# Half-array pairs in two bank-swapping phases for the dense products and transposes of an attention + mixer kernel

## The chip, the cores and the metric

The kernel runs on one core of a Trainium2 chip. The metric is the device time of one execution in microseconds; for the kernel before, the median of three runs is 702.48 us (701.95 to 702.92). The engines are named as the profile names them: PE is TensorE, the 128 x 128 array that multiplies a stationary matrix, loaded from 128 partitions, with a moving one of up to 512 columns into one of eight banks of PSUM (PEld is the loading); DVE is VectorE, ACT ScalarE, POOL GpSimd, and SP the queue that issues most DMAs.

## What is computed

Two blocks read the same normalized tokens `xn` (2048 x 512) and are added to `x`: a memory-augmented linear/softmax attention over four segments of 512 tokens, 32 heads of 16, and a mixer MLP with 1792 hidden columns.

```python
def _A_ref(x, wq, wk, wv, wo, beta):      # per segment s of 4, L = 512
    logits = einsum("bhqd,bhkd->bhqk", qs, ks) * scale + mask
    p = softmax(logits); a_dot = einsum("bhqk,bhkd->bhqd", p, vs)
    pq = phi(qs)                            # phi(t) = t + 1 if t > 0 else exp(t)
    a_mem = einsum("bhld,bhde->bhle", pq, M) / (einsum("bhld,bhd->bhl", pq, z)[..., None] + 1e-6)
    o = g * a_mem + (1.0 - g) * a_dot
    M = M + einsum("bhld,bhle->bhde", phi(ks), vs); z = z + einsum("bhld->bhd", phi(ks))
    ...
    return o @ wo
def _B_ref(x, w1, b1, w2, b2):
    return gelu(layernorm(x) @ w1 + b1) @ w2 + b2
x = A_x; xn = layernorm(x)
return x + _A_ref(xn, ...) + _B_ref(xn, ...)
```

## The kernel before

The work is cut into 16 units: segment s (of 4) times group g (of 4, eight heads each); unit i is s, g = divmod(i, 4). Large products are made of fp16 halves: a number is split into a high part and a remainder, and three products (high x high, high x low, low x high) are added in PSUM. `split3` (L469) does that for a full 128-row contraction in KT = 4 steps, 12 products for each result.

The jobs that the change and the prediction speak of:

- `T` (`qk_proj`, L469): query or key of a unit, 12 full-array products of 512 columns. Behind it ACT and DVE read the bank and split it into `hl`, five DMAs on SP send it to DRAM (`qd`, `kd`) and back into the stacked tiles `qst`, `kst`.
- `M` (`m_jobs`, L594 on PE, L601 on DVE): the score maxima. The eight heads of a unit lie in the two 64-row halves of the array, so the products come in pairs, one in each half, into two banks, and run at the same time. The maxima go to `mc`; `R` (`m_row`, L609) transposes them.
- `S` (`s_jobs`, L634 on PE, L639 on ACT): the scores again, in the same pairs, and their exponentials into `pt`. `pv` (L663) multiplies these with the values, in four strips of 32 columns of the array; `K` (`kv`, L573) sums the memory in the same strips. `Qd` (`a_mem`, L542) applies the memory.
- `V` (`v_nat`, L469), values of a segment, and `out` (L788), the output product: 12 full-array products of 512 columns for each 128 tokens.
- `D` (`d_jobs`, L469): first MLP product, for 256 tokens and 128 hidden columns 12 full-array products of 256 columns; DVE reads the result at L729. `e` (`e_part`, L769): second MLP product, already as half-array pairs. [...] 
- Transposes through PE with an identity: the tokens (`ln_tr`, L455), the keys (`pk_nat`, L505), the maxima (L609), the row scales (`ratio`, L428), each 128 x 128 or, for the maxima, 128 x 32.

Nothing here is scheduled at run time. `streams()` lists the jobs by kind, a long string `ORDER` names, letter by letter, from which list the next job comes, and each engine gets its instructions in that order. A second string, `BANKS`, gives the PSUM bank of each `dense()` call, one digit each. [...]

```python
ps = dense(), dense()                      # m_jobs: a pair, one product in each half of the rows
for b, p in enumerate(ps):
    r = slice(64 * b, 64 * b + KM)
    T.matmul(p[:, o:o + n], stk[i, 0][r, t, P * qb:P * qb + P], stk[i, 1][r, t, :n], start=True, stop=True)
```

## Time and profile before

| | us |
|---|---|
| median of three runs | 702.48 |
| the profiled execution | 701.74 |
| its span, first to last instruction | 700.0 |
| PE busy | 681.6 (97%) |
| PE busy, first 50 us | 40.0 |
| DVE busy | 536.2 (77%) |
| ACT busy | 515.4 (74%) |
| POOL busy | 349.5 (50%) |
| granted TensorE clock, mean | 0.995 |

A row of a group reads: line, engine, operation, what it writes <- what it reads, shape and count | busy us, mean ns of one | idle us of the engine before it, and what ended that. `64*128` is the part of the array that a product uses (rows x columns), `64x512` its moving operand. A row of the timeline reads: start, length, engine, line, operation; equal neighbours are merged with their count. Products overlap in the array, so their mean is longer than the distance between their starts. A row of stretches gives the busy time of PE, PEld, DVE, ACT and POOL, then the granted clock, the share of the DMA engines and GB/s.

### The profile page before, as it was taken

To read this page: it belongs to the slowest core of one execution; us is meant where nothing else is said; L and a number is where in the kernel's file an instruction comes from. 1 tells how busy PE (TensorE), PEld (TensorE's weight loads), DVE (VectorE), ACT (ScalarE), POOL (GpSimd) and SP (SyncE) were. 2 spreads that over 40 slices of the span, in tenths; PEclk is the share of its full clock that TensorE was granted. 3 is DMA by queue.
4 is the path that set the end of the run, shared out by engine and by line. 5 is a ranking of instruction groups with operands and counts; after the bars stand their busy time and mean duration, and the time that the engine had idled before them with its cause. 6 is when DMAs were issued, how large, how long until landed. Compare 5 with 4: busy or idle time off the path is not lost.

```text
span 700.0 us, 16681 instructions
## 1 busy us (share of the span) xinstructions
PE 681.6 (97%) x6213; PEld 395.4 (56%) x6213; DVE 536.2 (77%) x1734; ACT 515.4 (74%) x954; POOL 349.5 (50%) x532
## 2 busy tenths in 40 slices
PE   7799999999999999999999999999999999999997
PEld 6355556575554555666454456566454556556653
DVE  5699979797795858889689786979679585969533
ACT  6879897779785768667794698765886586887870
POOL 5276767465533435555434446354443345465652
PEclk9899999999999999999999999999999999999999
DMA  9796123230404022323113322041121204241001
GB/s 280 222 252 182 33 67 89 68 86 4 121 3 122 31 78 62 78 47 77 48 48 109 94 59 76 18 107 46 42 69 46 93 2 107 77 111 29 4 2 61
DMA packets 51790, 55.11 MB, mean 79 GB/s; under 512 B 4782, under 2 KB 40636, under 8 KB 51708
## 3 DMA queue, kind: packets, MB, share of 16 engines
q1 hardware_dynamic: 49404, 49.84, 25.6%
q0 software_dynamic: 2304, 4.20, 3.6%
q8 instruction: 49, 0.80, 0.4%
q14 instruction: 33, 0.27, 0.1%
HBM read 36.99 MB, written 17.04 MB: 77 GB/s over the span
## 4 chain that ended last, share of the span: by engine, by line
PE 71%; DVE 9%; ACT 8%; DMA 6%; POOL 2%; issue 2%; SPq 1%; POOLq 0%; ACTq 0%; DVEq 0%
PE ps L469 27%; PE ps L769 17%; PE ps L663 9%; PE ps L788 5%; PE ps L634 5%; PE ps L594 4%; DVE ps L601 3%; ACT pt L639 2%; DMA qd<-hl 1%; PE ps L542 1%; ACT hT L736 1%; DMA mhl<-in_B_b_dram 1%; ACT w1s L310 1%; SPq L251 1%; DMA wos<-in_A_wo_dram 1%
## 5 line engine op out<-in xcount | busy, mean ns | idle before, releaser
L601 DVE CUSTOM_DVE_ANT_0 ps<-ps,mask 128x512 f32<-128x512 f32 (+3 forms) x512 | 234.0, 524 | 10.1 <-PE ps L594 8.9
L639 ACT ACTIVATE pt<-ps,qkcs 128x512 f32<-128x512 f32 (+1 forms) x384 | 204.7, 626 | 26.2 <-PE ps L634 21.8
L769 PE MATMUL ps<-w2s,hT 64*128 64x512 f16 x1344 | 175.0, 375 | 0.6 <-DVE fence L772 0.5
L469 PE MATMUL ps<-xnT,w1s 128*128 128x256 f16 x1344 | 159.1, 273 | 0.7 <-DVE phq L499 0.4
L648 POOL TENSOR_SCALAR_AFFINE_SELECT pt<-pt 128x256 f32<-128x256 f32 x256 | 101.1, 426 | 107.5 <-ACT pt L639 107.3
L469 PEld LDWEIGHTS <-w1s 128*128 128x128 f16 x1344 | 128.6, 98 | 28.4 <-issue 10.3
L769 PEld LDWEIGHTS <-hT 64*128 64x128 f16 x1344 | 77.1, 94 | 54.6 <-issue 7.3
L745 POOL TENSOR_TENSOR hT<-hh,hT 128x512 f16<-128x512 f32 x64 | 68.0, 1062 | 75.0 <-ACT hT L744 75.0
L663 PE MATMUL ps<-pt,vt 128*32 128x256 f32 (+3 forms) x1024 | 77.3, 436 | 0.0
L729 DVE SCALAR_TENSOR_TENSOR hT<-ps,sc,sr 128x256 f32<-128x256 f32 x112 | 51.7, 478 | 30.1 <-PE ps L469 28.1
L601 DVE DVE_READ_ACCUMULATOR2_ANT mc<- 128x1 f32 x512 | 71.8, 140 | 0.0
L634 PE MATMUL ps<-qst,kst 50*128 50x512 f16 (+3 forms) x512 | 70.2, 298 | 0.7 <-DMA qst<-md 0.3
L594 PE MATMUL ps<-kst,qst 48*128 48x512 f16 (+3 forms) x512 | 67.4, 297 | 1.1 <-DMA qst<-qd 0.9
L744 ACT ACTIVATE hT<-hh 128x512 f16<-128x512 f32 x64 | 36.6, 573 | 39.9 <-POOL hh L743 39.5
L663 PEld LDWEIGHTS ps<-pt,vt 128*32 128x32 f32 x1024 | 30.5, 109 | 42.9 <-issue 33.4
L743 POOL TENSOR_SCALAR hh<-hT,sc 128x512 f32<-128x512 f32 x64 | 41.6, 651 | 25.0 <-ACT hT L736 23.2
L736 ACT ACTIVATE hT<-hT,b1t 128x256 f32<-128x256 f32 x112 | 46.4, 495 | 0.2
L489 DVE SCALAR_TENSOR_TENSOR hl<-ps,hl 128x512 f16<-128x512 f32 x32 | 22.1, 689 | 32.0 <-ACT phk L488 16.3
L469 PE MATMUL ps<-xnT,wks 128*128 128x512 f16 x192 | 46.0, 389 | 0.1
L469 PE MATMUL ps<-xnT,wqs 128*128 128x512 f16 x192 | 45.8, 390 | 0.2 <-DVE mc L601 0.2
L634 PEld LDWEIGHTS <-kst 50*128 50x128 f16 x512 | 27.8, 94 | 28.8 <-issue 13.6
L469 PE MATMUL ps<-wvs,xnT 128*128 128x512 f16 x192 | 44.0, 379 | 0.1
(220 smaller groups left out, 899.9 us busy)
## 6 DMA issues: line engine op xcount, KB each, us to landing
kd<-hl SPq DMA_DIRECT2D x48, 128.0 KB
kst<-kd SPq DMA_DIRECT2D x32, 192.0 KB
qd<-hl SPq DMA_DIRECT2D x48, 128.0 KB
qst<-qd SPq DMA_DIRECT2D x32, 192.0 KB
acc<-in_A_x_dram SPq DMA_DIRECT2D x16, 256.0 KB
acc<-in_B_b_dram POOLq DMA_DIRECT2D x16, 256.0 KB, 4.3
out_dram<-acc SPq DMA_DIRECT2D x16, 256.0 KB
xt<-in_A_x_dram SPq DMA_DIRECT2D x14, 256.0 KB
```

What stands on the lines that cost most here:

```text
L469: T.matmul(p, wsl(ws, k, a), xsl(xs, k, b), start=s0 and i == 0, stop=s1 and i == 3 * n - 1)
L594: T.matmul(p[:, o:o + n], stk[i, 0][r, t, P * qb:P * qb + P], stk[i, 1][r, t, :n], start=True, stop=True)
L601: V.tensor_tensor_reduce(p[:, o:o + n], p[:, o:o + n], mask[:, 512 - n:], 1.0, -3e38, OP.add, OP.max, mc[i][:, 4 * b + t, qb:qb + 1])
L634: T.matmul(p[:, o:o + n], stk[i, 1][r, t, P * kb:P * kb + P], stk[i, 0][r, t, P * kb:], start=True, stop=True)
L639: A.activation(e[:, OFF[kbs[0]]:OFF[kbs[0]] + o], p[:, :o], AF.Exp, scale=qkcs[:, 1, i % NG:i % NG + 1])
L648: G.affine_select(v, v, pattern=[[0, 2], [1, P]], compare_op=OP.is_ge, fill=0.0, base=0, channel_multiplier=-1)
L663: T.matmul(p[32 * c:32 * c + 32, P * kb:], vt[s, kb][:, 4 * g + c, 16 * odd:16 * odd + 32], pt[i, 2 * c + odd][:, OFF[kb]:OFF[kb] + LEN[kb ...
L729: V.scalar_tensor_tensor(hz[:, fi, :], p[:, :256], col(CG + fh), srow[hs][:, own], op0=OP.mult, op1=OP.mult)
L736: A.activation(z, z, AF.Gelu_apprx_tanh, bias=b1t[:, FH * (j % 2) + f:FH * (j % 2) + f + 1])
L743: G.tensor_scalar(t, hz[:, z, :], col(SHH + j % 2), 0.0, op0=OP.mult, op1=OP.add)
L745: G.tensor_tensor(hT[:, z, 1, :], t, hT[:, z, 0, :], op=OP.subtract)
L769: T.matmul(pes[j][a], hTs[fh][r, fi, u, P * a:P * a + P], w2s[r, fo, v, :], start=n == 0 and m == 0, stop=fi == FH - 1 and m == 2, skip_gr ...
```

## The change

From the second segment on, and for the second half of the first segment's MLP, the full-array jobs `T`, `V`, `out` (of the first three segments) and `D` become pairs of half-array products: `T2` makes key and query of a unit together, `V2` and `o2` two blocks of 128 tokens, `D2` two blocks of hidden columns. Each has two phases, which are jobs of their own with a letter each in `ORDER`; in the second the halves change banks. `swap` puts a wait for the last product of the first phase before the second, and takes the place of `fence` in `e_part` too. Transposes become pairs of 64 x 64 transposes into two banks (`turn`), each read out by itself; `mc` is 96 columns wide, so that its transposes use the array as 64 x 128 too. The buffer counts of `hl` (now 2) and `sr` (now 1) change, and `ORDER` and `BANKS` are new.

In the order of PE, at a border between value products and maxima of a middle unit, there stood before (names with the bank in front: ps0 is bank 0):

```order
L469 MATMUL ps0_3382<-wvs_101,xnT_2231 128x512
L469 LDWEIGHTS xnT_2231
L469 MATMUL ps0_3382<-wvs_101,xnT_2231 128x512
L594 LDWEIGHTS qst1_90
L594 MATMUL ps7_3396<-kst1_92,qst1_90 128x384 [waits Activation_49]
L594 LDWEIGHTS qst1_90
L594 MATMUL ps5_3397<-kst1_92,qst1_90 128x384 [waits DVE_49]
L594 LDWEIGHTS qst1_90
```

and at such a border now stand the end of a `V2` job's second phase, one maxima job, and the start of a `D2` job's second phase (L534 is the product in `halves`, L684 that of the maxima):

```order
L534 LDWEIGHTS xnT_5551
L534 MATMUL ps3_6605<-wvs_101,xnT_5551 128x512
L684 LDWEIGHTS qst1_90 [waits DMAHW4_49,DMAHW1_49]
L684 MATMUL ps5_6730<-kst1_92,qst1_90 128x512 [waits DVE_49]
L684 LDWEIGHTS qst1_90 [waits DMAHW5_49,DMAHW2_49]
L684 MATMUL ps7_6731<-kst1_92,qst1_90 128x512 [waits DVE_49]
L534 LDWEIGHTS w1s_103 [waits PE_49]
L534 MATMUL ps4_6654<-xnT_5551,w1s_103 128x256
L534 LDWEIGHTS w1s_103
L534 MATMUL ps0_6653<-xnT_5551,w1s_103 128x256
```

One bank and the full array became two banks and half-array pairs; the load that waits for PE is the `swap`, and the maxima job stands between the phases.

The second place, also on PE, is in the last segments, where a `D2` job gives its banks (3 and 4) on. L724 is the product of the scores:

```order
L534 MATMUL ps4_10547<-xnT_8608,w1s_103 128x256
L534 LDWEIGHTS w1s_103
L534 MATMUL ps3_10546<-xnT_8608,w1s_103 128x256
L724 LDWEIGHTS kst1_92
L724 MATMUL ps7_10641<-qst1_90,kst1_92 128x384 [waits DVE_49]
L724 LDWEIGHTS kst1_92 [waits PE_49]
L724 MATMUL ps1_10642<-qst1_90,kst1_92 128x384 [waits Activation_49]
...
L684 LDWEIGHTS qst0_89 [waits DMAHW2_49,DMAHW7_49]
L684 MATMUL ps6_10651<-kst0_91,qst0_89 128x512 [waits Activation_49]
L684 LDWEIGHTS qst0_89 [waits DMAHW3_49,DMAHW0_49]
L684 MATMUL ps3_10652<-kst0_91,qst0_89 128x512 [waits DVE_49]
```

Before, a `D` job ended with one bank to be read, and the maxima behind it took others:

```order
L469 LDWEIGHTS w1s_103
L469 MATMUL ps0_7077<-xnT_4708,w1s_103 128x256
L594 LDWEIGHTS qst1_90
L594 MATMUL ps6_7095<-kst1_92,qst1_90 128x512 [waits DVE_49]
L594 LDWEIGHTS qst1_90
L594 MATMUL ps4_7096<-kst1_92,qst1_90 128x512 [waits DVE_49]
L594 LDWEIGHTS qst1_90
L594 MATMUL ps2_7101<-kst1_92,qst1_90 128x384 [waits DVE_49]
```

Now bank 3 is asked for again after one score job.

The third place is on ACT, where transposes are read out at the start of a segment. Before:

```order
L430 ACTIVATE sr<-ps_4968 128x512
L458 ACTIVATE xnT<-ps_4975 128x4x128
L458 ACTIVATE xnT<-ps_4982 128x4x128
L507 ACTIVATE pkn<-ps_4989 128x512
L611 ACTIVATE mhl<-ps_4996 32x128
```

and now:

```order
L484 ACTIVATE xnT<-ps_5775 128x4x64
L484 ACTIVATE xnT<-ps_5776 128x4x64
L484 ACTIVATE xnT<-ps_5789 128x4x64
L484 ACTIVATE xnT<-ps_5790 128x4x64
L701 ACTIVATE mhl<-ps_5809 32x64
L701 ACTIVATE mhl<-ps_5810 32x64
L852 ACTIVATE hT_114<-hh 128x256
L587 ACTIVATE pkn<-ps_5840 128x4x64
L587 ACTIVATE pkn<-ps_5841 128x4x64
L452 ACTIVATE sr<-ps_5853 128x4x64
L452 ACTIVATE sr<-ps_5854 128x4x64
```

Each read of one bank became two of half its width. The diff, cut to its core:

```diff
@@ streams
+        if s:
+            for ph in range(2):
+                pairs[ph].append(("T2", i, ph))
+        else:
+            keys.append(("T", i, 1))
+            queries.append(("T", i, 0))
...
-        hid += [("D", j, f) for f in range(FH)]
+        if hf == 0:
+            hid += [("D", j, f) for f in range(FH)]
+        elif fh == 0:
+            for ph in range(2):
+                hid2[ph] += [("D2", hf, c, ph) for c in range(FH)]
...
 ORDER = (
-    "aaccatccucaccuveattecvvvvcvctttttuaaattauetwvdcwucvbfwvxstxxxwyxycxgyxccxxwwxohoywcyvoofxnicyiaitoizzsyyziozygo"
+    "cCCaactaccCtcDceeDDatDCacttaDeDtcataaDCcbtEccEcfdDFsFcFhctFDGFEGFFgtocFGcFfoGEFoooEFEGoGHHDiiigGoHiGEiGiHGstppI"
...
 def ratio(n):
+        srow[n] = sb.tile([P, SEG], F32, name="sr")
+        if n:
+            ps = dense(), dense()
+            for j in range(4):
+                for b in range(2):
+                    r = slice(64 * b, 64 * b + 64)
+                    T.transpose(ps[b][:, 64 * j:64 * j + 64], rat[r, 4 * n + j:4 * n + j + 1].broadcast_to([64, P]), ident[r, r])
...
-    def ln_tr(t, dst, c0):
+    def ln_tr(t, dst, c0, own):
+        if own:
+            for b, p in enumerate(turn(t, KT)):
+                p3 = p[:, :256].rearrange("p (k c) -> p k c", k=KT)
+                c = slice(c0 + 64 * b, c0 + 64 * b + 64)
+                A.activation(dst[:, :, 0, c], p3, AF.Copy, scale=1024.0)
+                V.scalar_tensor_tensor(dst[:, :, 1, c], p3, 1024.0, dst[:, :, 0, c], op0=OP.mult, op1=OP.subtract)
+            return
...
+    def swap(key):
+        w = T.nop()
+        tc.add_manual_dep(w.ins, ends[key], mybir.DependencyInfo(mybir.DependencyClass.Sync, mybir.DependencyReason.DATA),
+                          reason="the halves of the array change banks")
+    def turn(src, n):
+        ps = dense(), dense()
+        for k in range(n):
+            for b in range(2):
+                r = slice(64 * b, 64 * b + 64)
+                a = src[r, P * k:min(P * k + P, src.shape[1])]
+                T.transpose(ps[b][:a.shape[1], 64 * k:64 * k + 64], a, ident[r, r])
+        return ps
+    def halves(key, ps, ph, n, lhs, rhs):
+        if ph:
+            swap(key)
+        for k in range(n):
+            for m, (u, v) in enumerate(((0, 0), (0, 1), (1, 0))):
+                for b in range(2):
+                    a = b ^ ph
+                    r = slice(64 * b, 64 * b + 64)
+                    w = T.matmul(ps[a], lhs(a, k, u)[r], rhs(a, k, v)[r], start=ph == 0 and k == 0 and m == 0,
+                                 stop=ph == 1 and k == n - 1 and m == 2, skip_group_check=True)
+        ends[key] = w.ins.name
...
+    def qk_both(i, ph):
+        s, g = divmod(i, NG)
+        if ph == 0:
+            both[i] = dense(), dense()
+        halves(("T", i), both[i], ph, KT, lambda a, k, u: (wks, wqs)[a][:, g, u, P * k:P * k + P],
+               lambda a, k, v: xnT[s][:, k, v, :])
+        if ph:
+            qk_use(i, 1, both[i][0])
+            qk_use(i, 0, both[i][1])
...
-        hl = sb.tile([P, 2, 512], F16, name="hl")
+        hl = sb.tile([P, 2, 512], F16, name="hl", bufs=2)
...
+    def d_pair(hf, c, ph):
+        fs = ((0, 1), (2, 3), (4, 5), (6, 13), (7, 8), (9, 10), (11, 12))[c]
+        if ph == 0:
+            both["D", hf, c] = dense(), dense()
+        ps = both["D", hf, c]
+        halves(("D", hf, c), [p[:, :256] for p in ps], ph, KT, lambda a, k, u: WT["1"][:, fs[a], u, P * k:P * k + P],
+               lambda a, k, v: xnT[hs][:, k, v, own])
+        if ph:
+            for a in range(2):
+                d_use(hf, fs[a], ps[a])
...
     def e_part(j, n):
+        if n == FH:
+            swap(("e", j))
...
-        if n == FH - 1:
-            V.tensor_copy(fence, pes[j][1][:1, :1])
+        ends["e", j] = w.ins.name
```

`v_pair` and `out_pair` are built like `d_pair`, on `xnT` with `wvs` and on `oT` with `wos`; `pk_nat` and `m_row` call `turn` and read its two banks one after the other.

144 lines of the change are left out of this document (91 added, 53 removed).

## The prediction

> **What bounds the kernel now.** I read the page's head and its engine shares first, then the chain of waits by engine, then the granted clock by stretches of time.
>
> ```profile
> span 700.0 us, 16681 instructions
> ...
> PE 681.6 (97%) x6213; PEld 395.4 (56%) x6213; DVE 536.2 (77%) x1734; ACT 515.4 (74%) x954; POOL 349.5 (50%) x532
> ...
> PE 71%; DVE 9%; ACT 8%; DMA 6%; POOL 2%; issue 2%; SPq 1%; POOLq 0%; ACTq 0%; DVEq 0%
> ...
> 0.00:50.00 50.00, 40.02 (x269) 27.23 (x270) 35.37 (x121) 36.46 (x68) 25.06 (x39) 0.93 0.89 247
> 75.00:700.00 625.00, 616.72 (x5739) 354.08 (x5736) 476.44 (x1517) 455.47 (x842) 308.52 (x477) 1.00 0.24 61
> ```
>
> TensorE (PE) is the bound. It is busy 97% and holds 71% of the chain; idle time is mostly in the first 50 us, while weights arrive; after 75 us it idles 8.3 of 625 us. DVE and ACT are at 77% and 74%: near enough to become the bound in a dense stretch, not over the whole. The change is almost all on PE, so I need PE's own prices, from groups of products by shape and the timeline.
>
> ```profile
> L769 PE MATMUL ps<-w2s,hT 64*128 64x512 f16 x1344 | 175.0, 375 | 0.6 <-DVE fence L772 0.5
> L469 PE MATMUL ps<-xnT,w1s 128*128 128x256 f16 x1344 | 159.1, 273 | 0.7 <-DVE phq L499 0.4 <-DVE mc L601 0.2
> L469 PE MATMUL ps<-xnT,wks 128*128 128x512 f16 x192 | 46.0, 389 | 0.1
> ...
> 305.06 0.27 PE L609 MATMUL ps<-ident,mc 128*32 128x128 f32 x1
> 305.26 0.39 PE L594 MATMUL ps<-kst,qst 48*128 48x512 f16 x2
> 305.49 0.81 PE L769 MATMUL ps<-w2s,hT 64*128 64x512 f16 x6
> 306.14 0.38 PE L594 MATMUL ps<-kst,qst 48*128 48x384 f16 x4
> 306.45 5.41 PE L469 MATMUL ps<-xnT,w1s 128*128 128x256 f16 x48
> ...
> 581.61 2.76 PE L469 MATMUL ps<-xnT,wqs 128*128 128x512 f16 x12
> 584.21 1.04 PE L469 MATMUL ps<-xnT,w1s 128*128 128x256 f16 x8
> ...
> 331.01 1.04 PE L455 MATMUL ps<-ident,xt 128*128 128x128 f32 x8
> 331.88 0.60 PE L505 MATMUL ps<-ident,phk 128*128 128x128 f32 x4
> ```
>
> (Rows like the third, with 192 products each, stand there for wqs, wvs and wos.) The durations overlap, so what counts is from start to start. A full-array product of 256 columns takes (5.41 - 0.27)/47 = 0.109 us, one of 512 columns (584.21 - 581.61)/12 = 0.216, a full transpose (331.88 - 331.01)/8 = 0.109. A pair of half-array products of 512 columns (L769: one in each 64 rows, started together) takes (306.14 - 305.49)/3 = 0.217. So a half-array pair and a full product cost the same, and halving alone gains nothing. What costs is the change between the two. The pairs from 306.14 hold 384 + 128 = 512 columns and would be through at 306.36; the full product starts at 306.45: 0.09 lost. From the transpose at 305.06 to the half-array pair at 305.26 it is 0.20 instead of 0.109: again 0.09. Between L594 and L769, both half-array, nothing is lost. The starts of the trace say the same wherever the form changes: 0.205 for 0.109, 0.312 for 0.216. I take 0.095 us for a change.
>
> **The change part by part.** *Fewer changes of form: -9.9 us.* I counted along PE's order of both programs where neighbours differ in form (full; half rows, 64 x 128; four column strips, 128 x 32): 214 before, of which 140 between full and half, and 110 after, of which 30. The 104 fewer, at 0.095, are 9.9 us. Nothing else hides them: PE is the bound where they stand.
>
> *Dense products: 0, and +1.2 for small ones.* 288 of 384 query and key products, 144 of 192 value and 144 of 192 output products become pairs of 512 columns: 0.217 for 0.216. 1176 of the 1344 first-MLP products become pairs of 256 columns with two weight loads and two products in 0.109. The nearest rows are pairs of 256 columns in the score jobs:
>
> ```profile
> 155.82 0.45 PE L594 MATMUL ps<-kst,qst 48*128 48x384 f16 x4
> 156.48 0.29 PE L594 MATMUL ps<-kst,qst 48*128 48x256 f16 x2 [0.20 <-ACT pt L639]
> 156.59 0.38 PE L769 MATMUL ps<-w2s,hT 64*128 64x512 f16 x1
> ```
>
> The pair at 156.48 is followed after 0.11 us. Such spacings run from 0.108 to 0.114, the upper end with the job's own start in it, so 0 to 5 ns over 1176 pairs: 0 to +5.9. I take 1 ns, +1.2, since inside a job no start is paid.
>
> *Transposes: -6.1 us.* There are 144 full ones, 144 x 0.109 = 15.7 us. After it there are 20 (2.2 us) and 124 half-array pairs, each moving 64 columns instead of 128. No row has such a pair. If the moving side sets its time it takes half of 0.109, 0.055; if the load of the 128 columns of f32 does, it stays at 0.109. The total then lies between 9.0 and 15.7, a gain of 6.7 to 0. I take 0.06: in pairs of L594 and L769 the two halves' loads run at the same time, and 128-column pairs follow each other in 0.055.
>
> *The wait of phase two: +0.3.* The first load of the second phase waits for the end of the last product of the first, since both halves then write the other's bank. What such an end costs is seen where DVE waits for the last 256-column product of a job:
>
> ```profile
> 310.60 0.48 DVE L729 SCALAR_TENSOR_TENSOR hT<-ps,sc,sr 128x256 f32<-128x256 f32 x1 [0.71 <-PE ps L469]
> L772 DVE COPY fence<-ps 1x1 f32<-1x1 f32 x16 | 2.3, 145 | 6.0 <-PE ps L769 5.7
> ```
>
> The third job's last product started at 306.45 + 35 x 0.109 = 310.28; DVE started 0.32 later, 0.2 after the array was free. Behind the wait in PE's queue stands all of the second phase. So each of the 89 second phases loses up to 0.2 us, 17 in all, unless work stands between. In the order it does (another job of at least 0.21 us) in all but two that I could follow: 0.3 us. The old fence copies (16 on DVE, 2.3 us, with 0.5 of waiting on PE at L769) go: -0.5.
>
> *Reading out: +0.9.* What was one read of a bank becomes two of half the width.
>
> ```profile
> L507 ACT ACTIVATE pkn<-ps 128x512 f32<-128x512 f32 x12 | 7.2, 601 | 0.0
> ...
> L744 ACT ACTIVATE hT<-hh 128x256 f16<-128x256 f32 x16 | 6.7, 416 | 12.8 <-POOL hh L743 12.8
> L611 ACT ACTIVATE mhl<-ps 32x128 f16<-32x128 f32 x16 | 4.1, 259 | 9.1 <-PE ps L609 9.0
> L612 DVE SCALAR_TENSOR_TENSOR mhl<-ps,mhl 32x128 f16<-32x128 f32 x16 | 4.4, 273 | 2.0 <-ACT mhl L611 1.9
> ```
>
> ACT: 27 reads become two of 256 columns (2 x 0.416 - 0.60 = 0.23 more, 6.2 us), 16 of the row maxima become two (I take 0.2 for each half, +0.14, 2.3 us): 8.5 us. DVE: the same for 16 maxima and 12 of L459, about 4.4 us, less 2.3 of fences. By the chain's shares, 8% and 9%, 0.9 us of this is on the path; PE's products cover the rest. If that cover were gone it would be 10.6.
>
> *Query and key at once: 0.* The two products of a unit now end together, so their ten transfers stand on SP one after the other, and the first maxima job waits for the last. The path of such a one in the chain before:
>
> ```profile
> 104.49 5.03 DMA qd<-hl
> ...
> 109.96 3.65 DMA qst<-qd
> ```
>
> With the reading out before it that is about 11 us. In PE's work by the rows above, 10 to 16 us lay between the later product and the first maxima job of a unit, now 13 to 17. The added lead covers the queueing; without it each of 12 units would lose up to the 3.65 us of a second transfer.
>
> *Banks: +5.7.* This is the cost that speaks against the change. A pair holds two of the eight banks over both phases and the job between, twice as long for each output as one full product. A bank is free only when it has been read:
>
> ```profile
> L601 DVE CUSTOM_DVE_ANT_0 ps<-ps,mask 128x512 f32<-128x512 f32 x128 | 86.8, 719 | 5.9 <-PE ps L594 5.4
> L601 DVE DVE_READ_ACCUMULATOR2_ANT mc<- 128x1 f32 x512 | 71.8, 140 | 0.0
> L639 ACT ACTIVATE pt<-ps,qkcs 128x512 f32<-128x512 f32 x256 | 157.3, 696 | 15.7 <-PE ps L634 14.9
> ```
>
> I followed each bank along PE's order and called a reuse tight when PE's own work between the last product into it and the next is shorter than the 0.2 us above plus the reader's rows (0.86 for DVE, 0.70 for ACT, twice for the second bank of a pair, 0.7 elsewhere): 34 of some 1020 reuses before, 66 of 1058 after. For the price, the rows at 155.82 and 156.48 show one: 0.66 until the next start where 384 + 128 columns take 0.217, so 0.44 lost, with ACT's read named as its end. Over all waits of PE beyond 0.04 us after 50 us I add up 13.1 us in 74 places, 0.18 each. 32 more at 0.18 are 5.7. The lower bound is 0, new places that happen to be free; the upper one is in the rival on banks.
>
> The sum: -9.9 - 6.1 + 1.2 + 0.3 - 0.5 + 0.9 + 5.7 = -8.4 us. The profiled execution took 701.74 us (span 700.0 and 1.7 around it), 0.7 less than the 702.48 median, so 693.3 for such an execution and **694.1** for the median.
>
> **The rivals.** *Banks cost nothing more.* The new order was written for the new holding times, and DVE and ACT have 160 us free each. Then 5.7 falls away: 688.4. Against it, the tight places doubled.
>
> *Banks become the bound in dense stretches, and it is slower.* The place: two finished phases, then several score jobs in a row, as at bank 3 in the order shown, where DVE owes 0.48 per product read and 1.72 for each maxima pair while PE has 0.22 us of other work. The price: adding up all products and changes from the rows leaves 41 of 700 us, of which 15.5 lie in the first 50 us and about 6 at the ends, so 20 us is the most that PE lost elsewhere. If the 34 tight reuses made all of it, each costs 0.59, and 32 more 18.8 in place of 5.7: 707.2. It decides once an added reuse costs (8.4 + 5.7)/32 = 0.44 us. Against it: half of the 20 us has other names (loads from DMA, the change to the memory product). [...]
>
> *PE cannot issue twice as many instructions.* The densest long mix in the trace is a round of score jobs: 16 instructions for 512, 384, 256 and 128 columns in 0.217 + 0.162 + 0.110 + 0.055 = 0.54 us, 34 ns each. If that were the limit, a pair of the first MLP (4 instructions) would take 0.136, and 1176 x 0.027 = 31.8 us makes 725.9. Against it stands a stretch where the limit would show:
>
> ```profile
> 430.10 0.52 PE L573 MATMUL ps<-vt,pkn 128*32 128x48 f32 x32
> ```
>
> 32 products and their 32 loads are through in 0.52 us, 8 ns each, though some of them were queued. [...]
>
> *The forms don't merge everywhere.* If the transposes of the 96 maxima columns count as another form than the pairs beside them, 16 jobs pay two changes, 3.0 us: 697.1.
>
> **How the numbers follow.** The forecast has 0.53, no bank cost 0.20, banks as the bound 0.16, issue 0.05, forms 0.06. A measurement of this kernel tells 0.2% (1.4 us) from no change. Faster: 0.92 of the forecast, all of the second case, most of the last: 0.74. Slower: 0.21, within 0.2%: 0.05. The forecast's own range is 688 to 702. For 8 in 10 I take 685 (the full gain on transposes, no bank cost, a calmer start) to 707 (banks at their upper price), which leaves out the issue case and the upper half of the bank case.
>
> **What would show it.** In the new profile: pairs of 256 columns 0.109 to 0.114 us apart, 48 products in about 2.7 us; transpose pairs 0.055 to 0.06 apart; no 0.095 steps between score jobs and dense jobs. PE's busy time should fall to some 670 us, its share stay at 96 to 97%, and waits of L684 and L724 for DVE and ACT grow by some 6 us. [...] The prediction is wrong if PE's steps are as priced and the time still doesn't fall.

## The result, and the profile after

The changed kernel takes **722.06 us** (median of four runs, 719.66 to 726.8) against 702.7 us for the kernel before in the same set of runs: a ratio of 1.028, 95% interval 1.022 to 1.034. It is slower by 19 us. The forecast was 694.1 us, and the time lies above the whole range of 685 to 707.

The profiled execution took 723.07 us. The head of its page, engine shares, and the chain of waits by engine and by line:

```profile
span 721.4 us, 20439 instructions
...
PE 688.6 (95%) x8089; PEld 430.3 (60%) x8089; DVE 540.4 (75%) x1746; ACT 523.9 (73%) x998; POOL 350.9 (49%) x533
...
PE 54%; DVE 17%; ACT 12%; DMA 10%; issue 3%; SPq 2%; POOL 1%; DVEq 0%; ACTq 0%
PE ps L534 20%; PE ps L878 12%; DVE ps L691 7%; PE ps L753 6%; ACT pt L729 6%; PE ps L503 5%; PE ps L684 4%; PE ps L724 3%; DMA qst<-qd 3%; DMA qd<-hl 2%; DMA md<-mhl 1%; PE ps L896 1%; DVE mc L691 1%; DVE hT L825 1%; PE ps L622 1%
```

PE's share of the chain fell from 71% to 54%. DVE (9 to 17), ACT (8 to 12) and DMA (6 to 10) took what it lost: PE is no longer the one bound. PE's busy time rose, from 681.6 to 688.6, where about 670 was forecast. That figure misleads. A product counts as busy for all of its time in the array, so when starts lie further apart, the overlaps go and the busy time grows: the two groups below have a mean of about 300 ns in both kernels, and their busy time rises from 137.6 to 161.4 us together. Where the clock was at half (last section), a product of 256 columns also lasted longer, 0.42 us in place of 0.27. Starts tell more.

First the maxima and score products, grouped by line; behind the second bar stands PE's idle time ahead of them, and what ended most of it. Before the change:

```profile
L634 PE MATMUL ps<-qst,kst 50*128 50x512 f16 (+3 forms) x512 | 70.2, 298 | 0.7 <-DMA qst<-md 0.3 <-ACT nD L672 0.3
L594 PE MATMUL ps<-kst,qst 48*128 48x512 f16 (+3 forms) x512 | 67.4, 297 | 1.1 <-DMA qst<-qd 0.9 <-ACT pt L639 0.2
```

After it (L684 and L724 are the same products):

```profile
L724 PE MATMUL ps<-qst,kst 50*128 50x512 f16 (+3 forms) x512 | 82.0, 301 | 5.5 <-DMA qst<-md 3.4 <-ACT pt L729 1.0 <-DVE mc L691 0.3
L684 PE MATMUL ps<-kst,qst 48*128 48x256 f16 (+3 forms) x512 | 79.4, 300 | 9.9 <-DMA qst<-qd 4.3 <-ACT pt L729 2.3 <-DVE mc L691 1.8
```

1.8 us of idle time became 15.4, half of it ended by a DMA and much of the rest by ACT's and DVE's reads of score banks. The idle time is only the part in which the array was quite empty.

For the whole of it I laid the start of every product against the sum of the prediction's prices along PE's order (0.109 us for 256 columns, 0.216 for 512, 0.06 for a pair of half transposes, 0.095 for a change of form), and called what starts later a wait, named by what that product waits for in the program. The span is the work by the prices, the waits, and 5.5 or 5.6 us at the end, in every kernel here. In microseconds:

| profiled execution | before | after | difference |
|---|---|---|---|
| PE's work by the prices | 659.1 | 643.0 | -16.1 |
| waits in the first 50 us | 15.5 | 18.9 | +3.4 |
| later, a DMA among what is awaited | 1.5 (4 places) | 13.4 (24) | +11.9 |
| later, only ACT or DVE awaited (mostly a bank to be read) | 11.5 (69) | 25.3 (123) | +13.8 |
| later, nothing awaited (late all the same) | 2.5 | 10.5 | +8.0 |
| steps under 0.04 us, and waits for PE's own ends | 4.3 | 4.6 | +0.3 |
| span | 700.0 | 721.4 | +21.4 |

(The rows add up to 21.3; the rest is rounding.) So the work that was to go did go, and the waits doubled, from 35.3 to 72.8 us. In the fourth row, called waits for readers from here on, some 21 of the 25 us after the change and some 5 of the 11 before end within 0.15 us of the last read of the bank that the product writes. The rest end later, so they need not be waits for a bank: ACT or DVE may owe a value there.

**The prices held.** PE's timeline after the change, in a stretch where nothing was waited for:

```profile
180.75 0.28 PE L684 MATMUL ps<-kst,qst 48*128 48x256 f16 x2
180.86 1.48 PE L534 MATMUL ps<-xnT,w1s 64*128 64x256 f16 x24
...
187.62 2.78 PE L534 MATMUL ps<-xnT,w1s 64*128 64x256 f16 x48
190.24 0.81 PE L878 MATMUL ps<-w2s,hT 64*128 64x512 f16 x6
190.89 1.47 PE L534 MATMUL ps<-xnT,w1s 64*128 64x256 f16 x24
...
196.09 0.41 PE L522 MATMUL ps<-ident,phk 64*128 64x64 f32 x8
196.33 0.39 PE L724 MATMUL ps<-qst,kst 50*128 50x384 f16 x4
```

48 first-MLP products are 24 pairs: from 187.62 to 190.24 they take 2.62 us, 0.109 a pair. Three pairs of the second MLP take 190.89 - 190.24 = 0.65, 0.217 each, and the next job follows at once: no change of form is paid. A score pair of 256 columns is followed by the first MLP 0.11 later. Eight half transposes, four pairs, are through in 0.24: 0.06 a pair.

### The profile page after: what moved, and what is told of

The parts are those of the page before. It is cut to its first block, busy times and chain, and to the rows that moved or that the text cites. A ratio compares the mean times of both kernels' runs of the same rounds, so it can differ in the third digit from the quotient of the medians.

```text
span 721.4 us, 20439 instructions
## 1 busy us (share of the span) xinstructions
PE 688.6 (95%) x8089; PEld 430.3 (60%) x8089; DVE 540.4 (75%) x1746; ACT 523.9 (73%) x998; POOL 350.9 (49%) x533
## 4 chain that ended last, share of the span: by engine, by line
PE 54%; DVE 17%; ACT 12%; DMA 10%; issue 3%; SPq 2%; POOL 1%; DVEq 0%; ACTq 0%
PE ps L534 20%; PE ps L878 12%; DVE ps L691 7%; PE ps L753 6%; ACT pt L729 6%; PE ps L503 5%; PE ps L684 4%; PE ps L724 3%; DMA qst<-qd 3%; DMA qd<-hl 2%; DMA md<-mhl 1%; PE ps L896 1%; DVE mc L691 1%; DVE hT L825 1%; PE ps L622 1%
## 5 line engine op out<-in xcount | busy, mean ns | idle before, releaser
L534 PE MATMUL ps<-xnT,w1s 64*128 64x256 f16 x2352 | 149.2, 270 | 0.6 <-DVE mc L691 0.4
L534 PEld LDWEIGHTS <-w1s 64*128 64x128 f16 x2352 | 124.4, 94 | 17.8 <-issue 3.3
L684 PE MATMUL ps<-kst,qst 48*128 48x256 f16 (+3 forms) x512 | 79.4, 300 | 9.9 <-DMA qst<-qd 4.3
L724 PE MATMUL ps<-qst,kst 50*128 50x512 f16 (+3 forms) x512 | 82.0, 301 | 5.5 <-DMA qst<-md 3.4
L753 PE MATMUL ps<-pt,vt 128*32 128x512 f32 (+3 forms) x1024 | 77.5, 436 | 0.2
L534 PE MATMUL ps<-xnT,wks 64*128 64x512 f16 x288 | 66.1, 376 | 0.0
L534 PE MATMUL ps<-xnT,wqs 64*128 64x512 f16 x288 | 66.0, 376 | 0.0
L684 PEld LDWEIGHTS <-qst 48*128 48x128 f16 x512 | 34.3, 95 | 34.4 <-issue 12.9
L724 PEld LDWEIGHTS <-kst 50*128 50x128 f16 x512 | 35.6, 95 | 27.0 <-issue 7.8
L783 POOL TENSOR_TENSOR nN<-nN,oT 128x512 f32<-128x512 f32 x16 | 20.2, 1265 | 48.6 <-DVE oT L597 48.6
```

The costliest lines, as they stand in the source:

```text
L534: w = T.matmul(ps[a], lhs(a, k, u)[r], rhs(a, k, v)[r], start=ph == 0 and k == 0 and m == 0, stop=ph == 1 and k == n - 1 and m == 2, skip_ ...
L724: T.matmul(p[:, o:o + n], stk[i, 1][r, t, P * kb:P * kb + P], stk[i, 0][r, t, P * kb:], start=True, stop=True)
L753: T.matmul(p[32 * c:32 * c + 32, P * kb:], vt[s, kb][:, 4 * g + c, 16 * odd:16 * odd + 32], pt[i, 2 * c + odd][:, OFF[kb]:OFF[kb] + LEN[kb ...
```

## The experiments

Each kernel ran in three rounds beside the kernel before; "of before" is the ratio with its 95% interval. Names with `a` start from the changed kernel, names with `b` from the order of the kernel before.

### The transfers of query and key: `a_sp`, `a_nodma`

The timeline of SP, and PE's first wait, for one unit of the changed kernel:

```profile
432.95 0.58 SPq L572 DMA_DIRECT2D kd<-hl  x1
...
438.45 0.83 SPq L577 DMA_DIRECT2D kst<-kd  x2
439.38 0.58 SPq L572 DMA_DIRECT2D qd<-hl  x1
...
443.83 0.95 SPq L577 DMA_DIRECT2D qst<-qd  x2
...
447.98 0.39 PE L684 MATMUL ps<-kst,qst 48*128 48x512 f16 x1 [0.64 <-DMA qst<-qd]
```

The queries' writes start only at 439.38, right behind the read-back of the keys, which SP held until the keys' writes had landed (it waits for `kd<-hl` there for 3.5 us). From the first write to the second product of the first maxima pair, which is the one that waits longest, are 15 us. `a_sp` moves only SP's order; `qk_use` puts its reads back into `later`:

```diff
-            qk_use(i, 1, both[i][0])
-            qk_use(i, 0, both[i][1])
+            later = []
+            qk_use(i, 1, both[i][0], later)
+            qk_use(i, 0, both[i][1], later)
+            for d, src in later:
+                Q.dma_start(d, src)
```

> The changed kernel (722.1 us), with one thing moved: of the ten transfers of a unit's keys and queries, the six writes to DRAM are issued before the four reads back, so that the writes of the queries no longer stand on SP behind the reads of the keys. Theory A (the transfers of query and key, issued together, come late): in the trace of the change the wait of the first maxima or score product for a DMA is about 12 us of the 38.8 us that PE waits after 50 us, and the queries' writes are issued 6 us after the keys'; so 710 to 714. Theory B (banks: readers too slow for two banks held at once) and theory C (the order as such): within 2 us of 722.

Measured: 716.97 us, 1.020 of before (1.016 to 1.023), 5.1 us less than the change and between the two expectations. The same unit's timeline in `a_sp`:

```profile
427.95 0.59 SPq L575 DMA_DIRECT2D kd<-hl  x1
...
429.89 0.57 SPq L575 DMA_DIRECT2D qd<-hl  x1
...
432.29 0.83 SPq L555 DMA_DIRECT2D kst<-kd  x2
434.86 0.79 SPq L555 DMA_DIRECT2D qst<-qd  x2
...
441.96 0.38 PE L691 MATMUL ps<-kst,qst 48*128 48x512 f16 x2
```

The queries' reads start 6.9 us behind the first write instead of 10.9, and the first maxima pair starts without a wait. Waits with a DMA fell from 13.4 to 7.0 us, which bears out the 5.1 us, since the two intervals just touch; those left are mostly the row maxima on their way to the scores, and one unit of the first segment. `a_nodma` takes these away too:

```diff
-        for b in range(2):
+        for b in range(2 * (s == 0)):
             Q.dma_start(t[64 * b:64 * b + 48], d[4 * b:4 * b + 4]...)
...
-        for b in range(2):
+        for b in range(2 * (i < NG)):
             Q.dma_start(stk[i, 0][64 * b + KM:64 * b + KS], ...)
```

> The changed kernel (722.1 us) without the reads back from DRAM from the second segment on: keys, queries and row maxima are still computed and written to DRAM, but score and maxima products go on with the last rows of the first segment, and wait for no transfer. In the trace of the change PE waits 13.4 us after 50 us where a DMA is among what it waits for (before the change 1.5). If these are waits of their own: 706 to 711. If a bank wait stands behind each of them and takes its place: 717 or more.

Measured: 715.2 us, 1.017 (1.014 to 1.020), 6.9 us less than the change. Waits with a DMA are down to 3.9, but waits for readers alone rose from 25.3 to 28.0: behind some transfers stood a bank that was not read either. The result lies between the two expectations: of the 9.5 us of waits with a DMA that went, 6.9 reached the time.

### Half arrays or order: `a_full`, `a_noswap`

`a_full` keeps the new jobs, order, banks and reads and computes in each phase one full product:

```diff
-        if ph:
-            swap(key)
         for k in range(n):
             for m, (u, v) in enumerate(((0, 0), (0, 1), (1, 0))):
-                for b in range(2):
-                    a = b ^ ph
-                    r = slice(64 * b, 64 * b + 64)
-                    w = T.matmul(ps[a], lhs(a, k, u)[r], rhs(a, k, v)[r], ...)
+                T.matmul(ps[ph], lhs(ph, k, u), rhs(ph, k, v), ...)
```

> The changed kernel with its jobs, banks, reads and order, but in each phase of keys, queries, values, first MLP and output one full-array product into one of the two banks, in place of half-array pairs into both; no wait between the phases there. The prices of the prediction give PE 664.6 us of work in place of 643.0 (227 more changes of form). Theory C (order and banks cost, whatever the form): the time does not fall, 722 to 744, by how much of the 21.6 us the waits take in. A theory that the half arrays themselves cost (issue, double weight loads, waits between phases): waits go back to before's 35 us and the time falls to 707.

Measured: 732.27 us, 1.042 (1.040 to 1.045): 10.2 more than the change for 21.6 more work. Waits went from 72.8 to 59.4, not to 35. So of the work that the half arrays save in this order, about half reaches the time, and waits take the rest. And even with full products, and with more work for PE than the kernel before (664.6 against 659.1), this order waits 24 us longer than the old one. That is the larger part of the 37.5 us of waits that the change added.

`a_noswap` leaves each half in its bank (`a = b`, no wait).

> The changed kernel with each half of the array staying in its own bank in the second phase, and so without the wait between the phases (it computes wrong sums). If the waits between phases stand open (0.2 us in each of 89): down by up to 17 us, to 705. If they are covered, as forecast at 0.3 us: within 1.5 us of 722.

Measured: 722.61 us, 1.028 (1.025 to 1.031). The waits between phases are covered, as far as runs that lie 5 us apart can tell; by the starts of the changed kernel, waits for PE's own ends of over 0.04 us come to some 0.5 us after the first 50.

### Which bank: `a_lru`, `b_lru`, `b_lru_rebank`, `a_sp_rebank`

A job's banks go to the end of the list `free` behind the job that reads them out:

```diff
-    bank = iter("".join(BANKS))
+    free, held = list("01234567"), []
     def dense():
-        return dps.tile([P, 512], F32, name="ps" + next(bank), bufs=1)
+        held.append(free.pop(0))
+        return dps.tile([P, 512], F32, name="ps" + held[-1], bufs=1)
```

> The changed kernel with its order, but the table of banks replaced by a rule: each job takes the bank that was given back longest ago. If the table's choice of banks is what costs: at least 5 us faster. If it is the number of banks held, or something else than banks: between 720 and 726.

Measured: 743.86 us, 1.059 (1.055 to 1.062): waits for readers doubled, to 51.8 us. Neither expectation held. The rule goes by the order of the program, not by when a reader is through; the table does better.

`b_lru` puts the old `ORDER` and full products under the same rule (transposes and the wait of the second MLP stay as changed).

> The order of the kernel before, full products as before, with the changed kernel's half-array transposes and its wait between the second MLP's phases, and banks by the rule that cost 21.8 us in the changed order (taken is the one given back longest ago). PE's work by the rows: 655.8 us, 3.3 less than before. If the old order is as sensitive to the choice of banks as the new one: about 720. If it has slack in its banks (34 tight reuses against 66): 702 to 708.

Measured: 724.72 us, 1.030 (1.027 to 1.033): the old order is as sensitive. `b_lru_rebank` replaces the rule by a table from that run's own times (each output gets the bank that was free longest).

> The old order with full products and half-array transposes (724.7 us with the rule for banks), now with a table of banks made from its own measured times: each output gets the bank that was free longest. If the choice of banks made the rule's 22 us: 700 to 708. If not: 715 or more.

Measured: 710.40 us, 1.012 (1.008 to 1.015). 14 us of the rule's cost came back, not all 22. This kernel, on which the next experiments rest, has 3.3 us less work than the kernel before and is 7.5 us slower; whether its table or its added reads make that was not tried. The same done to the changed order, with `a_sp`'s transfers:

> The changed kernel with the queries' writes before the keys' reads (717.0 us), with a table of banks made from that run's own measured times. By those times the old table left 111 outputs without a free bank, the new one 99. If the table can be made much better: 712 or less. If all eight banks are in use in the places that wait: 714 to 720.

Measured: 714.38 us, 1.016 (1.013 to 1.019), beside 1.020 (1.016 to 1.023) for `a_sp`: the intervals overlap. A better table was not to be had from these times. In the changed kernel 79 of the 121 outputs that waited for a reader (20.2 of 25.1 us) found none of the eight banks free when their wait began; before the change 32 of 63 (5.7 of 10.1 us). (The other waits of the 123 and 69 stand at products that are not the first into their bank.)

### Two banks held over two phases: `b_pairs`, `b_pairs_rebank`, `b_7banks`, `a_full_rebank`

From the first product into a bank to the end of its last read, an output of the dense jobs held its bank for 3.62 us before (1.55 of it PE's), and for 7.13 after (5.16 PE's). Over all outputs 5.08 of eight banks were held on the average after 50 us, then 5.66. `b_pairs` has the pairs without the new order: in the old one, values, output and six sevenths of the first MLP as pairs, the two phases in the places of two successive jobs. Against the kernel before:

```diff
-            hid += [("D", j, f) for f in range(FH)]
+            hid += [("D2", hf, 3 * fh + c, ph) for c in range(3) for ph in range(2)] + [("D", j, FH - 1)]
```

> As the one before it (old order, banks by the rule), with values, output and six sevenths of the first MLP from the second segment on as half-array pairs: each phase stands where one of two successive full products stood; keys and queries stay full. PE's work by the rows: 653.4 us, of it 4.6 of waits between neighbouring phases. If a pair's banks cost nothing more than two full products': 2 to 3 us less than the one before it. If holding two banks over two phases is what costs, also without the new order: at least 5 us more than it.

Measured: 787.28 us, 1.119 (1.117 to 1.121), 63 more than `b_lru` for 2.4 less work. With a table from its own times:

> The old order with values, output and six sevenths of the first MLP as pairs (787.3 us with the rule for banks), with a table made from its own measured times in the same way. If only the choice of banks was bad: down by 50 us or more, near the one before it. If two banks held over two phases are the cost: above 750, since even the best assignment by these times leaves 79 outputs that find no bank free (the run of full products in this order: 25).

Measured: 762.44 us, 1.086 (1.084 to 1.087): still 52 more than `b_lru_rebank`. The phases lie further apart here, and a pair's output holds its bank for 10.25 us. The groups of `b_lru_rebank` and then of `b_pairs_rebank`, with the idle time ahead of the products:

```profile
L727 PE MATMUL ps<-qst,kst 50*128 50x512 f16 (+3 forms) x512 | 71.4, 298 | 0.8 <-DVE mc L694 0.4 <-ACT nD L765 0.2 <-DMA qst<-md 0.2
...
L687 PE MATMUL ps<-kst,qst 48*128 48x384 f16 (+3 forms) x512 | 69.3, 299 | 1.9 <-DMA qst<-qd 1.6
```

```profile
L537 PE MATMUL ps<-xnT,w1s 64*128 64x256 f16 x2016 | 126.2, 269 | 3.1 <-DVE mc L694 1.2 <-ACT pt L732 0.3
L727 PE MATMUL ps<-qst,kst 50*128 50x512 f16 (+3 forms) x512 | 80.1, 297 | 9.5 <-ACT pt L732 4.4 <-DVE mc L694 1.9 <-DVE phq L584 0.9
...
L687 PE MATMUL ps<-kst,qst 48*128 48x384 f16 (+3 forms) x512 | 74.7, 297 | 8.0 <-DVE mc L694 3.1 <-DVE nD L770 1.9 <-DVE hl L574 1.0
```

The score jobs wait, though nothing in them was changed, and they wait for reads of banks. Waits for readers are 17.0 us in the one and 61.7 in the other. `b_7banks` is `b_lru_rebank` with a table of seven banks.

> The old order with full products and half-array transposes and a table of banks made from its own measured times (710.4 us), with seven banks in place of eight; nothing else is changed. By the traces the pairs of the change hold 1041 bank microseconds after 50 us where the same kind of outputs held 543 before: 0.75 of a bank on the average. If a bank less is what the changed kernel suffers from: 15 to 30 us more than 710. If banks are not scarce: within 5 us of 710.

Measured: 747.76 us, 1.064 (1.061 to 1.067): 37 us for one bank, with full products and the old order, and more than the 15 to 30 that were expected. Its waits for readers are 54.0 us. A part can be the new table, since the choice of banks alone moved this order by 14 us. Still, banks are scarce already in the old order, and `b_pairs_rebank` shows that holding outputs longer costs there, without the new order.

`a_full_rebank` is `a_full` with the second bank of a pair taken only with the second phase, and a table from `a_full`'s times.

> The changed order with one full product in each phase (a_full, 732.3 us), but the second bank of a pair of outputs is taken only with the second phase, and the table of banks is written anew: each output gets the bank that was free longest by the times of a_full's trace. If the second bank, held empty over the first phase, is what makes PE wait for banks in this order: its waits for readers fall from 21.5 us to 12 to 15, and the time to 722 to 727. If the order makes the waits whatever is held: 730 or more.

Measured: 728.73 us, 1.037 (1.034 to 1.039), 3.5 less than `a_full` and between the two expectations; waits for readers fell from 21.5 to 19.6 only. In the new order the hold over the first phase is a small part.

`a_full_early` was to go further and read keys, queries, values and output right behind their own phase.

> As the kernel with full products in the changed order (a_full, 732.3 us), but keys, queries, values and output are each read right behind their own phase, as before the change, so that a finished bank is not held over the second phase and the keys' transfers start a phase earlier; the first MLP's stay as they are. PE's work by the rows is the same 664.6 us. If holding two banks over both phases and the late transfers are what the changed order lost: its waits for readers (21.5 us) and DMA (5.6) fall towards before's 11.8 and 1.5, so 720 to 724. If the order alone makes the waits: 729 or more.

Measured: 785.30 us, 1.116 (1.115 to 1.118), far above what either theory had foreseen. Waits with a DMA rose to 31.4 us, single ones to 8 us: an earlier read also moves the instructions behind it on ACT, DVE and SP, and the order no longer fits. It says nothing on banks.

### The readers: `a_short`, `a_shortms`, `a_short2`, `a_nodma_short`, `a_nodma_short2`

In a dense stretch of the changed kernel, PE's timeline:

```profile
500.15 0.39 PE L724 MATMUL ps<-qst,kst 50*128 50x384 f16 x4
500.74 0.27 PE L684 MATMUL ps<-kst,qst 48*128 48x256 f16 x1 [0.20 <-ACT pt L729]
501.32 0.27 PE L684 MATMUL ps<-kst,qst 48*128 48x256 f16 x1 [0.31 <-ACT pt L729]
```

and ACT's:

```profile
498.85 0.69 ACT L761 ACTIVATE nN<-ps,bg 128x512 f32<-128x512 f32 x1 [0.22 <-PE ps L753]
499.43 0.68 ACT L762 ACTIVATE nD<-ps,eo 128x512 f32<-128x512 f32 x1
500.00 3.73 ACT L729 ACTIVATE pt<-ps,qkcs 128x512 f32<-128x512 f32 x7
```

ACT works without a break from 498.85 on; at 500.00 it begins seven exponentials in a row, while PE is already through with the next scores and starts each product as a bank comes free. Of the 123 waits for readers, 67 (15.0 us) are like this: the reader had been busy without a break since before the data was ready. Before the change there were 34 (4.5 us). `a_short` halves DVE's side:

```diff
-  V.tensor_tensor_reduce(p[:, o:o + n], p[:, o:o + n], mask[:, 512 - n:], ...)
+  V.tensor_tensor_reduce(p[:, o:o + n // 2], p[:, o:o + n // 2], mask[:, 512 - n:512 - n // 2], ...)
```

> The changed kernel (722.1 us) with DVE's maxima read over the first half of the columns only (the other half is left out of the maxima). DVE saves about 100 us of work and gives the banks of the maxima jobs back earlier. If PE waits because banks are not read out in time: its waits for readers (25.3 us) fall by half or more, 706 to 713. If readers are not the limit and only the order or DMA is: 719 or more.

Measured: 718.67 us, 1.022 (1.019 to 1.025), close to the second expectation; the interval overlaps with that of the change (1.022 to 1.034). Where PE waits did move. Waits behind a busy DVE at the maxima's banks all but vanished (5.2 to 0.1 us), those behind a busy ACT grew from 8.7 to 11.7, and waits with a DMA from 13.4 to 16.0. `a_shortms` halves ACT's exponentials as well (`p[:, :o // 2]`) and lets GpSimd fill the rest.

> The changed kernel with both readers of the score jobs shortened: DVE takes the maxima over half of the columns, ACT the exponentials of half of the columns (GpSimd writes ones into the other half). DVE's half alone gave -3.4 us. If banks that are not read out in time make the 25 us of waits for readers: 708 to 714. If ACT's reads don't matter either: 717 or more.

Measured: 723.67 us, 1.029 (1.026 to 1.032), and `a_nodma_short`, the same without the reads back:

> Both at once: no reads back from DRAM from the second segment on, and both readers of the score jobs over half of the columns. The prices of the prediction give PE 643.0 us of work here, and 7 us stand around it; before the change PE lost 35 us beside its work. If DMA and banks together are all that was lost: 643 + 7 + some 35 to 40 = 685 to 690. If something else is lost that neither explains: 700 or more.

Measured: 715.45 us, 1.018 (1.016 to 1.020). Both fit the second expectation, and taken alone they would have sunk the theory. But the value products now wait for GpSimd, as their group in `a_shortms` shows:

```profile
L754 PE MATMUL ps<-pt,vt 128*32 128x256 f32 (+3 forms) x1024 | 84.2, 436 | 1.6 <-POOL pt L739 1.6
```

By starts these products lose 7.5 us there, and some 3 or less in the kernels without the filling. The experiment had put a new cost in the place of the one that it removed. `a_short2` shortens the same reads with no new work: four lasting buffers in turn, whose second half keeps old values.

```diff
-  pt[i, 4 * b + t] = sb.tile([P, 1280], F32, name="pt", bufs=4)
+  pt[i, 4 * b + t] = next_pt()
...
-  A.activation(e[:, OFF[kbs[0]]:OFF[kbs[0]] + o], p[:, :o], AF.Exp, ...)
+  o2 = o // 2 if i >= NG else o
+  A.activation(e[:, OFF[kbs[0]]:OFF[kbs[0]] + o2], p[:, :o2], AF.Exp, ...)
```

> The changed kernel (722.1 us), its maxima and (from the second segment on) its exponentials read over half of the columns as in a_shortms, but with no filling by GpSimd: four lasting buffers for the exponentials are used in turn, and the other half keeps old values. If readers that are behind are a cause of their own (15 us of PE's waits end when a busy DVE or ACT has read a score bank): 706 to 713. If another chain (DMA, the readers' own waits) ends at almost the same time in these places: 717 or more, with other names in the waits.

Measured: 709.05 us, 1.010 (1.007 to 1.014): 13.0 less than the change. And without the reads back:

> The same without the reads back from DRAM from the second segment on. If transfers and readers are the two causes and nothing else stands behind them: 685 to 695 (643 us of work, 7 around it, 35 to 45 of waits as before the change). If it stays above 705, the waits lie in the order itself.

Measured: 699.07 us, 0.9955 (0.9934 to 0.9975): 23.0 less than the change, and 4 above the range for the case that nothing else stands behind the two. The groups of `a_short2`, then engine shares and chain of `a_nodma_short2`:

```profile
L730 PE MATMUL ps<-qst,kst 50*128 50x512 f16 (+3 forms) x512 | 78.5, 300 | 5.8 <-DMA qst<-md 4.2 <-ACT pt L736 0.5 <-DVE phq L587 0.3
...
L690 PE MATMUL ps<-kst,qst 48*128 48x512 f16 (+3 forms) x512 | 77.3, 299 | 6.1 <-DMA qst<-qd 5.2 <-DVE mc L697 0.3
```

```profile
PE 674.9 (96%) x8089; PEld 411.3 (59%) x8089; DVE 465.0 (66%) x1746; ACT 475.6 (68%) x998; POOL 350.0 (50%) x533
...
PE 77%; ACT 7%; DVE 7%; DMA 3%; POOL 2%; issue 2%; SPq 0%; DVEq 0%; ACTq 0%
```

With short reads the names of ACT and DVE all but leave the idle time of these groups, and the DMAs stay; by the starts, waits for readers fall to 14.4 us. With both gone PE has 77% of the chain. Alone the two are worth 6.9 and 13.0 us, together 23.0: their effects add, and the 3 us above the sum lie within the spread of the runs. (The last kernel is no rival of the kernel before, whose readers were not shortened. Nor are the 13.0 us the price of the change alone: the same shortening was not tried on the kernel before, which has 11.5 us of waits for readers itself.) The waits of the main kernels side by side, in us, as in the first table:

| kernel | work | first 50 us | DMA | readers | nothing awaited | span |
|---|---|---|---|---|---|---|
| before | 659.1 | 15.5 | 1.5 | 11.5 | 2.5 | 700.0 |
| after | 643.0 | 18.9 | 13.4 | 25.3 | 10.5 | 721.4 |
| `a_sp` | 643.0 | 17.9 | 7.0 | 26.9 | 9.2 | 714.3 |
| `a_nodma` | 643.0 | 18.4 | 3.9 | 28.0 | 8.7 | 712.3 |
| `a_short2` | 643.0 | 19.6 | 14.3 | 14.4 | 6.4 | 707.9 |
| `a_nodma_short2` | 643.0 | 20.8 | 5.0 | 15.6 | 5.1 | 699.5 |
| `a_full` | 664.6 | 18.7 | 5.6 | 21.5 | 7.4 | 729.5 |
| `b_lru_rebank` | 655.8 | 15.6 | 3.2 | 17.0 | 5.4 | 707.6 |
| `b_pairs_rebank` | 653.4 | 16.0 | 5.8 | 61.7 | 12.6 | 760.8 |
| `b_7banks` | 655.8 | 16.1 | 2.5 | 54.0 | 5.3 | 744.5 |

None of these kernels that computes the whole result beats the kernel before.

## Why the prediction was wrong, point by point

- **Fewer changes of form, transposes, small pairs** (-9.9, -6.1, +1.2): right, and the small pairs cost nothing that shows (0.109). Added up over every instruction by the same prices the work falls by 16.1 us, and the timeline shows these prices. What failed is the step from work to time. "PE is the bound where they stand" was read from the kernel before, and for what the new order makes PE wait the sum had 5.7 us for banks and nothing for transfers. `a_full` shows two parts. With full products, and more work for PE than before, the new order already waits 24 us longer. The other 13 come when PE has 21.6 us less to do, and meets readers and transfers with as much to do as before. How much of the 24 is the order itself, and how much is outputs held, read and sent in pairs, stays open; `a_full_rebank` gives 3.5 us to the second bank.
- **The wait of phase two** (+0.3): `a_noswap` agrees, within its spread. The fences (-0.5) were not tried alone.
- **Reading out** (+0.9): the added work was as forecast on ACT (515.4 to 523.9 us, +8.5) and 2 us above on DVE (536.2 to 540.4, +4.2 against 2.1). The price was wrong: the chain's share before (8% and 9%) was taken for the chance that a read stands on the path. After the change ACT and DVE hold 29% of the chain, and halving their reads of the score banks is worth 13 us (`a_short2`). Those reads stood there before; what the added ones cost by themselves no run shows.
- **Query and key at once** (0): wrong, by 5 us that SP's order alone gave back and some 7 with all transfers gone. Of the 11.9 us in the table of waits, some 7 are at the maxima, which wait for query and key, and some 4 at the scores, which wait for the row maxima's own transfers; those stood in no term. The step that failed is "the added lead covers the queueing". It set 13 to 17 us of lead against about 11, the path of one transfer alone. The ten transfers took 15 in the unit shown, since the queries' writes stood on SP behind a read that waits for the keys' writes to land. The bound written beside it, up to 3.65 us a unit, would have allowed for this.
- **Banks** (+5.7): wrong in its size, 13.8 us in the table. The price of one wait was nearly right (0.18; 25.3/123 = 0.21 now). The count was not: 54 more waits, not 32. The criterion for a tight reuse let the reader begin as soon as the data was there, and took PE's work without its waits. But more than half of the waiting (15.0 of 25.3 us) is behind a reader that is still busy with earlier banks. A single reuse that looked loose became tight where the reader was several reads behind, as ACT was with seven exponentials in a row at 500.00.
- **The rivals.** "Banks become the bound in dense stretches" (707.2, given 0.16) named the mechanism. Its price of 18.8 us against 13.8 was fair; its place was partly wrong, since most of the waiting is for banks of the score jobs themselves (11.1 us behind ACT's reads and 7.7 behind DVE's, of 25.3), and it lacked the transfers and the clock. `a_short2`, with shorter reads of these banks, bears the mechanism out with 13.0 us. PE's issue and forms that don't merge were not it: pairs at 0.109, and no change paid in the rows above.
- **What was in no term**: +8.0 us with nothing awaited, about half of it at a lower clock (below), and +3.4 in the first 50 us, where only four pairs of half transposes stand among full products. All kernels in the new order lose 18 to 21 us there, those in the old one 15.5 to 17.6, so it belongs to the new order of the first segment; why was not tried.

PE's share hardly shows the case: it is 95%, where 96 to 97% was expected. The prediction's last sentence caught it: steps as priced, and no fall of the time.

Open: whether an order with longer leads for the transfers and score jobs further apart could turn the 16 us of work into time. No kernel here had one.

## What to carry to other kernels

The engine that was busy 97% here had 16.1 us of work less, and then waited 25.7 us longer for engines at 75% and for transfers: before counting such a saving, lay their queues of reads against the shorter work, job by job, and not each read by itself. Where a change comes with a new order, run that order with the old products first: here 24 of 37.5 us of added waits were in it. Where results are held longer, price the buffer by taking one away from the kernel that exists (here 37 us for one of eight), which needs only a new table. Where the writes and reads of two outputs come to stand together on one queue, as on SP here, all the writes should stand before the first read back (5.1 us in `a_sp`).

## What the runs showed of the hardware

**Behind a stretch with little work the clock was at half.** From 152 to 155 us PE started two products in the changed kernel, and those behind them ran at half speed. PE's timeline there:

```profile
152.64 0.39 PE L684 MATMUL ps<-kst,qst 48*128 48x512 f16 x1 [0.91 <-DMA qst<-qd]
153.41 0.39 PE L684 MATMUL ps<-kst,qst 48*128 48x512 f16 x1 [0.38 <-DMA qst<-qd]
155.20 1.23 PE L724 MATMUL ps<-qst,kst 50*128 50x512 f16 x5 [1.40 <-DMA qst<-md]
...
156.88 2.63 PE L534 MATMUL ps<-xnT,w1s 64*128 64x256 f16 x22
159.23 0.42 PE L724 MATMUL ps<-qst,kst 50*128 50x256 f16 x1
```

22 first-MLP products, 11 pairs, take 159.23 - 156.88 = 2.35 us, 0.214 a pair, twice the 0.109 of the other stretches. The granted clock falls from 1.00 to 0.50 at 154.4 us, 0.6 behind the end of the second of the two products, and is at 1.00 again from 161.2. The windows of 25 us from 150, before and after, with the granted clock ahead of the last two columns:

```profile
150.00:175.00 25.00, 24.49 (x262) 14.48 (x257) 21.16 (x82) 24.15 (x48) 13.71 (x25) 1.00 0.11 26
```

```profile
150.00:175.00 25.00, 22.19 (x260) 14.12 (x258) 18.56 (x75) 17.81 (x35) 11.79 (x18) 0.86 0.29 81
```

0.14 of 25 us are 3.5 us. After 50 us the changed kernel has three such windows (0.93, 0.86, 0.93), 7 us of clock in all, the kernel before none. Not all of it is lost, since PE also waits in these stretches: by the starts some 4 of the 10.5 us in which nothing was awaited lie in them. Where the rest comes from is not shown. In the other two windows the clock is at 0.50 from 55.4 to 58.8 and from 618.6 to 622.0 us, again behind waits of PE (0.80 us before 53.89, 0.75 before 615.53). Not every wait had this behind it: in the kernel before, PE was idle for 1.43 us up to 176.70, and the clock stayed at 1.00. In the three places the waits cost more than themselves, by some 4 us together.

**A waiting product started 0.05 us after the reader's end.** In some 60 of the changed kernel's 78 waits for readers of over 0.1 us, PE's start lies 0.05 us behind the recorded end of the last read of that bank (for a maximum, of the accumulator read behind it): the exponential or maximum that frees it is on the path to its very end.
